# Retention decays moved from q, k and the mask to the values and the result, and the instruction order planned anew

## Chip, cores and metric
One core of a Trainium2 chip. The metric is the device time of one execution in microseconds; the kernel before took 385.36 us (median of 3 runs, 385.14 to 385.75).

## What is computed
Three parts follow each other. Two batches, eight heads of 64, 768 tokens, a model width of 512.

```python
# 1. retention: a state with a decay for each head
gamma = 1.0 - 2.0 ** (-5.0 - np.arange(H))
for t in range(S):
    state = gamma * state + k[:, :, t] (outer) v[:, :, t]
    y[:, :, t] = scale * q[:, :, t] @ state
# 2. spectral mixing
theta = x @ w_theta
zr, zi = x * cos(theta), x * sin(theta)
u = x + w_tok_r @ zr + w_tok_i @ zi            # over the tokens
x2 = u + relu(u @ w_ch)
# 3. gated MLP with a product over the tokens
h = gelu(x2 @ w_in); a, v = halves of h
v_n = (v - mean) / sqrt(var + 1e-6) * g_ln
out = x2 + (a * (w_sg @ v_n + b_sg)) @ w_out
```

## The kernel before
**Tiling.** The 768 tokens of a batch are six chunks of 128; chunk `i` runs from 0 to 11 over both batches, `c` from 0 to 5 in one batch. All large products (angles, mixing, channels, MLP) are done in three terms: each operand is split into an upper part (ScalarE, `split_hi`, L302) and a remainder (VectorE, `split_lo`, L308), and `terms3` multiplies upper by upper, remainder by upper and upper by remainder.

**Retention of one chunk** (`retention`, L426). `load_qk` and `load_kv` bring 512 KB each. `scores` makes k times q for eight heads in two PSUM banks. VectorE multiplies them with a mask that holds scale, decay and causality (L456), scales k by its decay (`fade_k`, L468) and q by its decay, which comes as a block `dqs` of 256 KB for each chunk after the first (L477, L484). `outer` makes k times v, `grow` adds it to the state. `attend` sums the state's part, from the scaled q, and the chunk's part, from the masked scores and v. ScalarE copies the result from PSUM into `xa` or `xb` (L555), and it is split.

**Angles** (`theta`, L576). Twelve products over the four quarters of the model width give the angles of a chunk; the first two quarters use the packed weight `W_THETA`, the last two the weight behind it. ScalarE and VectorE make cosine and sine, PE turns the chunk (`turn`, L650), VectorE multiplies (L658), and the product `z` is split for the token mixing (`mix_main`, `mix_rest`).

**Weights** (`weight`, L343). Each packed weight of 1 MB is loaded into one of two raw buffers, unpacked by ScalarE (L361) and VectorE (L370, L381) and split.

**Order.** Nothing runs in the order of the text. Each step is entered in a `Plan` with an engine, an assumed duration, the buffers it reads and writes and a due time (`prio`). `schedule` (L92) goes through assumed time and gives each engine the ready step with the smallest due time within a short look; the instructions are then issued in that order on each engine, and transfers all from SyncE. The due times come from the constants `C` (L203): chunk `i` is due at `8 + DEL + 13 i`, retention up to `LEAD` earlier, angles `LT` later, mixing `LM` later. `PA` and `AHEAD` bound how far a step may go ahead of its due time. Up to 90 products of `ident` with itself (`keep_warm`, L1109) fill PE in assumed time until 34 us where nothing else is ready.

Of the kernel before, what the change touches and what calls it, by code (L numbers as in the profile page):

```python
# [10 lines left out]
F32 = mybir.dt.float32  # L11
# [21 lines left out]
W_THETA, W_MAIN, W_REST, W_CH, W_INV, W_INU, W_OUT = 0, 2, 8, 11, 13, 15, 17  # L33
N_WP = 19

RAWS, PAIRS, ONES = 2, 35, 7


class Buf:
# [21 lines left out]
class Plan:  # L61
# [5 lines left out]
    def __init__(self, room):  # L67
        self.ops, self.res, self.room = [], {}, room

    def op(self, eng, dur, fn, r=(), w=(), prio=0.0, port=False, after=(), until=None):  # L70
        deps, bufs = set(after), []
        for x in r:
            deps.update(self.res.setdefault(x, ([], []))[0])
        for x in w:
            ws, rs = self.res.setdefault(x, ([], []))
            deps.update(ws)
            deps.update(rs)
        for x in (*r, *w):
            b = x.whole if isinstance(x, Half) else x[0] if isinstance(x, tuple) else x
            if isinstance(b, Buf) and b not in bufs:  # L80
                bufs.append(b)
        o = Op(eng, dur, fn, deps, bufs, prio, port, until)
        for x in r:
            self.res[x][1].append(o)
        for x in w:
            self.res[x] = ([o], [])
        for b in bufs:
            b.users.append(o)
        self.ops.append(o)
        return o  # L90

    def schedule(self, look):  # L92
# [5 lines left out]
        rank, level = {}, {}  # L98
        for k, o in enumerate(self.ops):
            o.missing, o.out = len(o.deps), []  # L100
            level[o] = max([o.prio, *(level[d] for d in o.deps)])
            rank[o] = k
            for d in o.deps:
                d.out.append(o)
# [95 lines left out]
        return sorted(order, key=lambda o: (o.start, rank[o]))  # L200


C = dict(TC=13, LATE=60, AHEAD=20, LM=17, LT=2, LR=16, LW=12, LRW=0, PEL=0.1, DVEL=0.05, ACTL=0.4, CHP=0, SGP=25, RW2=1, PA=30, DEL=6, RS=3.8, LEAD=30, TH=-8, WARM=34.0, NWARM=90, GP=12, LEAD1=15)  # L203


@with_exitstack
def retention_spectral_gmlp(
# [2 lines left out]
    qkv: bass.AP,  # L210
    wts: bass.AP,
    wsg: bass.AP,
    dmask: bass.AP,
    dqs: bass.AP,
    decays: bass.AP,
    gvec: bass.AP,
# [39 lines left out]
    mv = const.tile([P, 3, 4, 2], F32, name="mv")  # L256
    rstd = const.tile([P, 3, 3, 4], F32, name="rstd")
    stats = const.tile([P, 2, 6], F32, name="stats")
    masks = const.tile([P, 2, 512], F32, name="masks")
    dk = const.tile([P, NCH, H], F32, name="dk")  # L260
    states = [const.tile([P, NP * D], F32, name=f"state{n}") for n in range(2)]
    V.memset(states[0], 0.0)
# [23 lines left out]
        return plan.op("PE", dur, fn, **k)  # L286

    def act(words, fn, ps=False, **k):
        return plan.op("ACT", (0.16 if ps else 0.21) + words * 0.83e-3, fn, **k)

    def dve(words, fn, ps=False, fast=False, **k):
        dur = 0.15 + words * (0.52e-3 if fast else 1.042e-3)
# [5 lines left out]
    def dma(kb, fn, **k):  # L298
        return plan.op("SP", kb / 410.0, fn, **k)
# [126 lines left out]
    def retention(i):  # L426
        b, c = divmod(i, NCH)
        t = early(i)
        E, eng = (V, dve) if i < C["GP"] else (G, pool)
        load_qk(i)  # L430
        load_kv(i)
        qk, kv = load[i, 0], load[i, 1]
        if i == 0:
            dma(
                512,
                lambda: nc.sync.dma_start(out=masks, in_=dmask),  # L436
                w=["masks"],
                prio=t - 11.5,
            )
            dma(6, lambda: nc.sync.dma_start(out=dk, in_=decays), w=["dk"], prio=t - 11.2)  # L440
        sc = [bank(), bank()]

        def scores():
# [4 lines left out]
                    cols = slice(p * P, (p + 1) * P)  # L448
                    mm(ap(sc[h])[:, cols], k[rows, cols], q[rows, cols], True, True)

        pe(0.93, scores, r=[qk], w=sc, prio=t)
        at[i] = Buf("pair")
        for h in range(2):

            def mask(h=h):
                V.tensor_tensor(  # L456
                    out=ap(at[i])[:, h * 512 : (h + 1) * 512],
                    in0=ap(sc[h]),
                    in1=masks[:, h],
                    op=ALU.mult,  # L460
                )

            dve(512, mask, ps=True, r=[sc[h], "masks"], w=[(at[i], h)], prio=t + 1)
        if c < NCH - 1:

            def fade_k(G=E):
                k3 = ap(kv)[:, 0:512].rearrange("p (h d) -> p h d", h=H)
                G.tensor_tensor(  # L468
                    out=k3, in0=k3, in1=dk[:, c, :, None].to_broadcast([P, H, D]), op=ALU.mult
                )  # L470

            eng(512, fade_k, r=[kv, "dk"], w=[(kv, 0)], prio=t + 1)
        if c > 0:
            dq, qd = Buf(), Buf()
            dma(
                256,
                lambda: nc.sync.dma_start(out=ap(dq), in_=dqs[c - 1]),  # L477
                w=[dq],
                prio=t - 8,
                after=[gate[i - 2]] if i >= 2 else (),  # L480
            )
            eng(
                512,
                lambda: E.tensor_tensor(  # L484
                    out=ap(qd), in0=ap(qk)[:, 0:512], in1=ap(dq), op=ALU.mult
                ),
                r=[qk, dq],
                w=[qd],
                prio=t + 1.5,
            )  # L490
        state, state_next = states[c % 2], states[(c + 1) % 2]
        if c < NCH - 1:
            kp = bank()

            def outer():
                kk, vv = ap(kv)[:, 0:512], ap(kv)[:, 512:1024]
                for p in range(NP):
                    for h in range(2):
                        rows = slice(h * D, (h + 1) * D)
                        cols = slice(p * P + h * D, p * P + (h + 1) * D)  # L500
                        mm(ap(kp)[rows, p * D : (p + 1) * D], kk[:, cols], vv[:, cols], True, True)

            pe(0.5, outer, r=[(kv, 0), kv], w=[kp], prio=t + 2)

            def grow():
                add = ap(kp)[:, 0 : NP * D]
                if c == 0:
                    V.tensor_copy(out=state_next, in_=add)
                else:
                    V.tensor_tensor(out=state_next, in0=add, in1=state, op=ALU.add)  # L510

            dve(
                256,
                grow,
                ps=True,
                r=[kp] + ([("state", c % 2)] if c else []),
                w=[("state", (c + 1) % 2)],
                prio=t + 2.5,
            )
        xp = bank()  # L520

        def attend():
            vv, a = ap(kv)[:, 512:1024], ap(at[i])
            if c > 0:
                for p in range(NP):
                    cols = slice(p * P, (p + 1) * P)
                    for h in range(2):
                        rows = slice(h * D, (h + 1) * D)
                        mm(
                            ap(xp)[rows, cols],  # L530
                            state[rows, p * D : (p + 1) * D],
                            ap(qd)[rows, cols],
                            p == 0,
                            False,
                        )
# [9 lines left out]
                        c == 0 or p == NP - 1,  # L545
                    )

        r = [kv, (at[i], 0), (at[i], 1)]
        if c > 0:
            r += [qd, ("state", c % 2)]  # L550
        gate[i] = pe(0.93 if c == 0 else 1.85, attend, r=r, w=[xp], prio=t + 3)
        keys = [("x", b, c, d) for d in range(NP)]
        act(
            512,
            lambda: A.activation(  # L555
                out=x_chunk(i),
                in_=ap(xp).rearrange("p (n t) -> p n t", n=NP),
                func=AF.Copy,
            ),
            ps=True,  # L560
            r=[xp],
            w=keys,
            prio=t + 5,
        )
# [11 lines left out]
    def theta(i):  # L576
# [1 line left out]
        t = T(i) + C['LT']  # L578
        th = bank()

        def angle():
            xh, xl = (ap(x, F32R) for x in xhl[i])
            terms3(
                ap(th),
                [
                    (
                        (xh[:, k * P : (k + 1) * P], xl[:, k * P : (k + 1) * P]),
                        w_tile(W_THETA + k // 2, k % 2),
                    )
                    for k in range(NP)  # L590
                ],
            )

        pe(
            2.75,
            angle,
            r=[*xhl[i], *wp[W_THETA], *wp[W_THETA + 1]],
            w=[th],
            prio=t,
        )  # L600
        kk = Buf(dtype=I32)
        z, zh, zl = Buf("pair"), Buf("pair", F32R), Buf("pair", F32R)
        co, r = Half(z, 0), Half(z, 1)
# [47 lines left out]
                    out=ap(tp)[:, p * P : (p + 1) * P], in_=x_chunk(i)[:, p], identity=ident  # L651
                )

        pe(0.5, turn, r=keys, w=[tp], prio=t + 5.3)

        def times():
            z2 = ap(z).rearrange("p (n t) -> p n t", n=2)
# [466 lines left out]
def _decays():  # L1124

    g = 1.0 - 2.0 ** (-5.0 - np.arange(H, dtype=np.float64))
    t = np.arange(P, dtype=np.float64)
    scale = 1.0 / math.sqrt(D)  # L1130
    m = np.zeros((P, 2, 512), np.float64)
    dq = np.zeros((NCH - 1, P, 512), np.float64)
    dk = np.zeros((P, NCH, H), np.float64)
    low = (t[None, :] >= t[:, None]).astype(np.float64)
    dist = np.maximum(t[None, :] - t[:, None], 0.0)
    for p in range(NP):
        cols = slice(p * P, (p + 1) * P)
        for h in range(2):
            gh = g[2 * p + h]
            m[:, h, cols] = scale * low * gh**dist  # L1140
            for c in range(NCH):
                dk[:, c, 2 * p + h] = gh ** (P - 1.0 - t - P * (c + 1.0))
                if c:
                    dq[c - 1, h * D : (h + 1) * D, cols] = scale * gh ** (t + 1.0 + P * c)
    return m.astype(np.float32), dq.astype(np.float32), dk.astype(np.float32)


def _tok_tiles(w):
# [66 lines left out]
```

## Time and profile before
| | |
|---|---|
| median of 3 runs | 385.36 us |
| the profiled execution | 385.82 us |
| its span, first to last instruction | 384.0 us |
| granted clock of TensorE, mean | 0.999 |
| busy: PE, VectorE, ScalarE | 378.7, 276.5, 167.6 us |
| bytes read from memory | 38.43 MB |

PE's busy time counts products that compute nothing (`keep_warm`) too. Start times below are microseconds from the span's start.

### The profile page before, as it was taken

Reading aid. Unit: us, or ns where it says so; the run is one execution under the profiler, and the core shown is the slowest. Engines: PE = TensorE matmul, PEld = TensorE weight load, DVE = VectorE, ACT = ScalarE, POOL = GpSimd, SP = SyncE. Lnnn points to the kernel's source line nnn. Section 1 sums busy time; section 2 is a strip of 40 time slices with the busy share of each in tenths; the row PEclk is TensorE's granted clock in tenths of the full one; section 3 lists DMA queues with packets and bytes.
Section 4 is the critical chain, followed back from the end, with each engine's and each line's share of the span. In section 5 each row is a group of like instructions: output and inputs, shape, how many; then the busy total and the mean of one; then the engine's idle time right before and its main releaser. Section 6 shows DMA issues by size and latency. Waiting matters only on the chain.

```text
span 384.0 us, 5887 instructions
## 1 busy us (share of the span) xinstructions
PE 378.7 (99%) x2456; PEld 322.8 (84%) x2456; DVE 276.5 (72%) x412; ACT 167.6 (44%) x240; POOL 3.0 (1%) x8
## 2 busy tenths in 40 slices
PE   8899999999999999999999999999999999999996
PEld 8887888887988988788898888888888888998885
DVE  2888998988988836698835555989799996554222
ACT  1437566655624444567123213777685812111000
POOL 0000000000000000000000000020000000000000
PEclk9999999999999999999999999999999999999999
DMA  7995545634267530008000000540000000000223
GB/s 293 408 366 224 219 153 203 249 157 145 111 218 247 191 111 3 2 12 342 4 0 2 0 0 16 172 184 2 0 0 2 0 1 2 0 2 29 109 86 106
DMA packets 11786, 41.95 MB, mean 109 GB/s; under 512 B 1520, under 2 KB 2544, under 8 KB 9328
## 3 DMA queue, kind: packets, MB, share of 16 engines
q1 hardware_dynamic: 11760, 41.58, 28.9%
q8 instruction: 19, 0.31, 0.3%
q14 instruction: 7, 0.06, 0.0%
HBM read 38.43 MB, written 3.15 MB: 108 GB/s over the span
## 4 chain that ended last, share of the span: by engine, by line
PE 94%; DMA 3%; SPq 1%; issue 0%; DVE 0%
PE b L283 93%; DMA b<-qkv 3%; PE b L650 1%; SPq L348 0%; SPq L416 0%; SPq L405 0%; DVE b L1029 0%; SPq L440 0%; SPq L436 0%
## 5 line engine op out<-in xcount | busy, mean ns | idle before, releaser
L283 PE MATMUL b<-b,b 128*128 128x512 f32 (+2 forms) x1788 | 332.5, 352 | 0.0
L283 PEld LDWEIGHTS b<-b,b 128*128 128x128 f32 (+1 forms) x1788 | 278.0, 183 | 47.8 <-issue 2.6
L302 ACT ACTIVATE b<-b 128x1024 fp32r<-128x1024 f32 (+1 forms) x64 | 54.1, 863 | 57.2 <-DVE b L977 35.5
L308 DVE TENSOR_TENSOR b<-b,b 128x512 fp32r<-128x512 f32 (+1 forms) x64 | 59.0, 945 | 12.4 <-ACT b L302 11.2
L381 DVE SCALAR_TENSOR_TENSOR b<-b 128x1024 int32<-128x1024 int32 x38 | 46.5, 1223 | 0.8
L361 ACT ACTIVATE b<-b 128x1024 f32<-128x1024 f32 x19 | 22.2, 1166 | 11.8 <-DMA b<-wts 11.8
L302 ACT ACTIVATE b<-xa 128x512 fp32r<-128x512 f32 x24 | 14.9, 629 | 22.3 <-DVE xa L779 12.0
L308 DVE TENSOR_TENSOR b<-xa,b 128x512 fp32r<-128x512 f32 x24 | 16.3, 689 | 11.2 <-ACT b L302 11.1
L283 PE MATMUL b<-b 64*128 64x128 f32 (+1 forms) x352 | 20.4, 258 | 1.1 <-DMA b<-qkv 1.1
L283 PEld LDWEIGHTS b<-b 64*128 64x128 f32 (+1 forms) x352 | 17.3, 164 | 4.8 <-issue 3.1
L456 DVE TENSOR_TENSOR b<-b,masks 128x512 f32<-128x512 f32 x24 | 15.6, 684 | 6.6 <-PE b L283 6.6
L791 ACT ACTIVATE b<-b 128x512 f32<-128x512 f32 x24 | 13.8, 591 | 13.1 <-PE b L283 12.2
L658 DVE TENSOR_TENSOR b<-b,b 128x1024 f32<-128x1024 f32 x12 | 14.6, 1221 | 6.3 <-PE b L650 6.3
L815 DVE SCALAR_TENSOR_TENSOR b<-b,b 128x512 f32<-128x512 f32 x24 | 15.9, 678 | 2.1 <-ACT b L809 2.0
L809 ACT ACTIVATE b<-b 128x512 f32<-128x512 f32 x24 | 14.6, 627 | 4.4 <-DVE b L799 4.4
L799 DVE SCALAR_TENSOR_TENSOR b<-b,b 128x512 f32<-128x512 f32 x24 | 15.5, 675 | 1.3 <-ACT b L791 1.3
L970 DVE SCALAR_TENSOR_TENSOR b<-b,gcol,brow 128x512 f32<-128x512 f32 x12 | 9.0, 749 | 10.1 <-PE b L283 9.9
L992 DVE TENSOR_TENSOR b<-b,xa 128x512 f32<-128x512 f32 x8 | 5.5, 691 | 14.2 <-PE b L283 14.2
L302 ACT ACTIVATE b<-xb 128x512 fp32r<-128x512 f32 x12 | 7.4, 631 | 18.0 <-DVE xb L737 9.5
L370 DVE TENSOR_SCALAR b<-b 128x1024 int32<-128x1024 int32 x19 | 13.1, 688 | 2.3 <-DMA b<-wts 2.3
L606 ACT ACTIVATE b<-b 128x512 int32<-128x512 f32 x12 | 7.2, 597 | 16.3 <-PE b L283 16.3
L626 ACT ACTIVATE b<-b 128x512 f32<-128x512 f32 x12 | 7.5, 628 | 13.3 <-DVE b L615 13.3
(49 smaller groups left out, 178.2 us busy)
## 6 DMA issues: line engine op xcount, KB each, us to landing
b<-wts SPq DMA_DIRECT2D x19, 1024.0 KB, 5.2
b<-qkv SPq DMA_DIRECT2D x24, 512.0 KB, 6.5
out<-b SPq DMA_DIRECT2D x11, 256.0 KB, 2.0
b<-dqs SPq DMA_DIRECT2D x10, 256.0 KB, 6.7
b<-wsg SPq DMA_DIRECT2D x9, 256.0 KB, 7.7
masks<-dmask SPq DMA_DIRECT2D x1, 512.0 KB, 4.1
brow<-bvec SPq DMA_DIRECT2D x1, 384.0 KB, 4.9
out<-b SPq DMA_DIRECT2D x2, 128.0 KB, 1.7
```

Source lines behind the costliest of these rows:

```text
L283: nc.tensor.matmul(out=o, lhsT=l, rhs=r, start=start, stop=stop)
L302: act(words, lambda: A.activation(out=hi(), in_=src(), func=AF.Copy), prio=prio, r=r, **k)
L308: lambda: E.tensor_tensor(out=lo(), in0=src(), in1=hi().bitcast(F32), op=ALU.subtract),
L361: lambda: A.activation(out=words(1).bitcast(F32), in_=words(1).bitcast(F32), func=AF.Copy, scale=REBIAS),
L370: lambda: V.tensor_scalar(out=words(0), in0=words(0), scalar1=29, scalar2=None, op0=ALU.logical_shift_right),
L381: lambda scalar=scalar, op=op: V.scalar_tensor_tensor(out=words(0), in0=words(1), scalar=scalar, in1=words(0), op0=op, op1=ALU.bitwise_or,),
L456: V.tensor_tensor(out=ap(at[i])[:, h * 512 : (h + 1) * 512], in0=ap(sc[h]), in1=masks[:, h], op=ALU.mult,)
L658: V.tensor_tensor(out=z2, in0=ap(tp)[:, None, :].to_broadcast([P, 2, 512]), in1=z2, op=ALU.mult)
L791: lambda: A.activation(out=ap(s), in_=ap(t), func=AF.Square),
L799: lambda: V.scalar_tensor_tensor(out=ap(s), in0=ap(s), scalar=1.0 / GA, in1=ap(t), op0=ALU.add, op1=ALU.mult),
L809: lambda: A.activation(out=ap(s), in_=ap(s), func=AF.Tanh, scale=GA * GC),
L815: lambda: V.scalar_tensor_tensor(out=ap(o), in0=ap(s), scalar=1.0, in1=ap(t), op0=ALU.add, op1=ALU.mult),
```

## The change
The decays leave q, k and the mask. The values of a chunk are scaled by `g ** -t`, with `t` counted from the start of the batch, before both `outer` and `attend`; the result is multiplied by `scale * g ** t`, a block `dqs` of 256 KB that is now loaded for all six chunks, the first included. The mask is one causal block of 128x128, made on the chip (two GpSimd instructions) and repeated over the heads by its access pattern; the load of 512 KB goes. For chunks 0 to 7 (`FA=8`) ScalarE scales the values, in eight instructions, one for each head; for 8 to 11 VectorE does it in one. VectorE makes the result from PSUM where ScalarE copied it. The angle products stand as two steps, each of which waits for its own weight alone. There is one more pair buffer (36). Assumed durations, `C` and the meaning of a step's level (`lev`) are new, so the order is.

```diff
-C = dict(TC=13, LATE=60, AHEAD=20, LM=17, LT=2, LR=16, LW=12, LRW=0, PEL=0.1, DVEL=0.05, ACTL=0.4, CHP=0, SGP=25, RW2=1, PA=30, DEL=6, RS=3.8, LEAD=30, TH=-8, WARM=34.0, NWARM=90, GP=12, LEAD1=15)
+C = dict(TC=13, LATE=90, AHEAD=60, LM=28, LT=9, LR=16, LW=15, LRW=15, PEL=0.1, DVEL=0.1, ACTL=0.7, CHP=5, SGP=10, RW2=0, PA=25, DEL=6, RS=3.8, LEAD=40, TH=-8, WARM=34.0, NWARM=90, FA=8, LEAD1=5)
...
-    masks = const.tile([P, 2, 512], F32, name="masks")
+    causal = const.tile([P, P], F32, name="causal")
+    G.memset(causal, 1.0)
+    G.affine_select(
+        out=causal, in_=causal, pattern=[[1, P]], compare_op=ALU.is_ge, fill=0.0, base=0,
+        channel_multiplier=-1,
+    )
...
-        pe(0.93, scores, r=[qk], w=sc, prio=t)
+        pe(1.06, scores, r=[qk], w=sc, prio=t)
...
-                    in1=masks[:, h],
+                    in1=causal[:, None, :].to_broadcast([P, NP, P]),
...
-            eng(512, fade_k, r=[kv, "dk"], w=[(kv, 0)], prio=t + 1)
...
+        def fade_v():
+            v3 = ap(kv)[:, 512:1024].rearrange("p (h d) -> p h d", h=H)
+            V.tensor_tensor(
+                out=v3, in0=v3, in1=dk[:, c, :, None].to_broadcast([P, H, D]), op=ALU.mult
+            )
+        def fade_v_heads():
+            for h in range(H):
+                v = ap(kv)[:, 512 + h * D : 512 + (h + 1) * D]
+                A.activation(out=v, in_=v, func=AF.Copy, scale=dk[:, c, h : h + 1])
+        k = dict(r=[kv, "dk"], w=[(kv, 1)], prio=t + 1)
+        if i < C["FA"]:
+            plan.op("ACT", 1.95, fade_v_heads, **k)
+        else:
+            dve(512, fade_v, **k)
...
-        act(
-            512,
-            lambda: A.activation(
+        dve(
+            512,
+            lambda: V.tensor_tensor(
                 out=x_chunk(i),
-                in_=ap(xp).rearrange("p (n t) -> p n t", n=NP),
-                func=AF.Copy,
+                in0=ap(xp).rearrange("p (n t) -> p n t", n=NP),
+                in1=ap(dq).rearrange("p (n t) -> p n t", n=NP),
+                op=ALU.mult,
             ),
...
+        for half in range(2):
+            def angle(half=half):
...
+            pe(1.37, angle, r=[*xhl[i], *wp[W_THETA + half]], w=[th], prio=t + 0.01 * half, lev=t)
```

## Rows read from the trace of the kernel before

**Rows 1.** The page, busy time of each engine.
```profile
PE 378.7 (99%) x2456; PEld 322.8 (84%) x2456; DVE 276.5 (72%) x412; ACT 167.6 (44%) x240; POOL 3.0 (1%) x8
```
**Rows 2.** Chain of waits in order of time: start, duration, what.
```profile
4.54 13.44 DMA b<-qkv
...
172.08 208.89 PE b L283 x1068
```
**Rows 3.** Waits of PE's weight loads, 24 to 381 us: total, times, longest.
```profile
PEld b L283 <- issue: 5.9, 27, 0.4
```
**Rows 4.** PE's timeline, 0 to 50 us: start, duration, line, operands, count.
```profile
4.92 1.16 PE L283 MATMUL b<-b 64*128 64x128 f32 x16
6.01 2.05 PE L283 MATMUL b<-ident 128*128 128x128 f32 x16
...
11.07 5.97 PE L283 MATMUL b<-ident 128*128 128x128 f32 x52
18.11 1.78 PE L283 MATMUL b<-b 64*128 64x128 f32 x32 [1.07 <-DMA b<-qkv]
19.82 2.50 PE L283 MATMUL b<-ident 128*128 128x128 f32 x20
...
23.34 0.49 PE L283 MATMUL b<-ident 128*128 128x128 f32 x2
23.76 1.09 PE L283 MATMUL b<-b,state 64*64 64x128 f32 x16
...
26.27 3.02 PE L283 MATMUL b<-b,b 128*128 128x512 f32 x12
...
38.40 8.46 PE L283 MATMUL b<-b,b 128*128 128x512 f32 x36
```
**Rows 5.** Windows of the head: busy of each engine, clock, DMA share, GB/s.
```profile
10.00:20.00 10.00, 8.93 (x101) 8.46 (x99) 8.16 (x11) 3.84 (x4) 0.00 (x0) 1.00 1.02 409
```
**Rows 6.** VectorE's timeline, 0 to 48 us.
```profile
7.73 0.69 DVE L468 TENSOR_TENSOR b<-b,dk 128x512 f32<-128x512 f32 x1 [0.33 <-DMA b<-qkv]
...
19.07 1.22 DVE L308 TENSOR_TENSOR b<-b,b 128x1024 fp32r<-128x1024 f32 x1
...
22.88 1.22 DVE L308 TENSOR_TENSOR b<-b,b 128x1024 fp32r<-128x1024 f32 x1
...
39.62 1.23 DVE L308 TENSOR_TENSOR b<-b,b 128x1024 fp32r<-128x1024 f32 x1 [0.34 <-ACT b L302]
```
**Rows 7.** ScalarE's timeline, 0 to 48 us.
```profile
11.44 1.22 ACT L361 ACTIVATE b<-b 128x1024 f32<-128x1024 f32 x1 [1.05 <-DMA b<-wts]
16.72 1.18 ACT L361 ACTIVATE b<-b 128x1024 f32<-128x1024 f32 x1 [4.06 <-DMA b<-wts]
...
31.38 0.60 ACT L555 ACTIVATE xa<-b 128x512 f32<-128x512 f32 x1
31.87 0.72 ACT L633 ACTIVATE b<-b,halfpi 128x512 f32<-128x512 f32 x1
```
**Rows 8.** Windows: busy PE, PEld, DVE, ACT, POOL, clock, DMA share, GB/s.
```profile
30.00:60.00 30.00, 30.00 (x250) 24.08 (x248) 28.98 (x36) 19.23 (x27) 0.00 (x0) 1.00 0.51 195
```
**Rows 9.** Instructions by line and shape: count, busy us, mean ns, idle before.
```profile
L302 ACT ACTIVATE b<-b 128x1024 fp32r<-128x1024 f32 x31 | 34.5, 1119 | 21.7 <-DVE b L381 9.0 <-DVE b L658 7.4 <-PE b L283 3.1
L302 ACT ACTIVATE b<-b 128x512 fp32r<-128x512 f32 x33 | 19.5, 624 | 35.5 <-DVE b L977 35.5
L456 DVE TENSOR_TENSOR b<-b,masks 128x512 f32<-128x512 f32 x24 | 15.6, 684 | 6.6 <-PE b L283 6.6
...
L900 ACT ACTIVATE b<-b,rstd 128x512 f32<-128x512 f32 x12 | 8.8, 805 | 3.8 <-DVE rstd L889 3.8
L633 ACT ACTIVATE b<-b,halfpi 128x512 f32<-128x512 f32 x12 | 8.7, 725 | 0.4
...
L468 DVE TENSOR_TENSOR b<-b,dk 128x512 f32<-128x512 f32 x10 | 6.8, 684 | 0.3 <-DMA b<-qkv 0.3
...
L555 ACT ACTIVATE xa<-b 128x512 f32<-128x512 f32 x8 | 4.8, 600 | 16.3 <-PE b L283 16.2
```

More of the change, by code (lines that the diff above doesn't have):

```diff
@@ L34 @@
 N_WP = 19
-RAWS, PAIRS, ONES = 2, 35, 7
+RAWS, PAIRS, ONES = 2, 36, 7
 class Buf:
@@ L68, in __init__, with op @@
         self.ops, self.res, self.room = [], {}, room
-    def op(self, eng, dur, fn, r=(), w=(), prio=0.0, port=False, after=(), until=None):
+    def op(self, eng, dur, fn, r=(), w=(), prio=0.0, port=False, after=(), until=None, lev=None):
         deps, bufs = set(after), []
@@ L82, in op @@
         o = Op(eng, dur, fn, deps, bufs, prio, port, until)
+        o.lev = prio if lev is None else lev
         for x in r:
@@ L100, in schedule @@
             o.missing, o.out = len(o.deps), []
-            level[o] = max([o.prio, *(level[d] for d in o.deps)])
+            level[o] = max([o.lev, *(level[d] for d in o.deps)])
             rank[o] = k
@@ L212, in retention_spectral_gmlp @@
     wsg: bass.AP,
-    dmask: bass.AP,
     dqs: bass.AP,
@@ L288, in act @@
     def act(words, fn, ps=False, **k):
-        return plan.op("ACT", (0.16 if ps else 0.21) + words * 0.83e-3, fn, **k)
+        dur = 0.21 + words * 0.83e-3 if words < 1024 else 0.085 + words * 1.06e-3
+        return plan.op("ACT", dur - (0.04 if ps else 0.0), fn, **k)
     def dve(words, fn, ps=False, fast=False, **k):
@@ L428, in retention @@
         t = early(i)
-        E, eng = (V, dve) if i < C["GP"] else (G, pool)
         load_qk(i)
@@ L433, in retention @@
         if i == 0:
-            dma(
-                512,
[L436 to L440, printed above, removed]
+            dma(6, lambda: nc.sync.dma_start(out=dk, in_=decays), w=["dk"], prio=t - 11.5)
         sc = [bank(), bank()]
@@ L456, in mask @@
                 V.tensor_tensor(
-                    out=ap(at[i])[:, h * 512 : (h + 1) * 512],
-                    in0=ap(sc[h]),
-                    in1=masks[:, h],
+                    out=ap(at[i])[:, h * 512 : (h + 1) * 512].rearrange("p (n t) -> p n t", n=NP),
+                    in0=ap(sc[h]).rearrange("p (n t) -> p n t", n=NP),
+                    in1=causal[:, None, :].to_broadcast([P, NP, P]),
                     op=ALU.mult,
                 )
-            dve(512, mask, ps=True, r=[sc[h], "masks"], w=[(at[i], h)], prio=t + 1)
@@ L464, in retention @@
[L464 to L470, printed above, removed]
-            eng(512, fade_k, r=[kv, "dk"], w=[(kv, 0)], prio=t + 1)
[L473 to L480, printed above, removed]
-            )
[L482 to L490, printed above, removed]
+            dve(512, mask, ps=True, r=[sc[h]], w=[(at[i], h)], prio=t + 1)
@@ L491, in retention @@
+        if i < C["FA"]:
+            plan.op("ACT", 1.95, fade_v_heads, **k)
+        else:
+            dve(512, fade_v, **k)
+        dq = Buf()
+        dma(
+            256,
+            lambda: nc.sync.dma_start(out=ap(dq), in_=dqs[c]),
+            w=[dq],
+            prio=t - 8,
+            after=[gate[i - 2]] if i >= 2 else (),
+        )
         state, state_next = states[c % 2], states[(c + 1) % 2]
@@ L501, in outer @@
                         mm(ap(kp)[rows, p * D : (p + 1) * D], kk[:, cols], vv[:, cols], True, True)
-            pe(0.5, outer, r=[(kv, 0), kv], w=[kp], prio=t + 2)
+            pe(0.58, outer, r=[(kv, 1), kv], w=[kp], prio=t + 2)
             def grow():
@@ L531, in attend @@
                             state[rows, p * D : (p + 1) * D],
-                            ap(qd)[rows, cols],
+                            ap(qk)[rows, cols],
                             p == 0,
@@ L546, in attend @@
                     )
-        r = [kv, (at[i], 0), (at[i], 1)]
+        r = [kv, (kv, 1), (at[i], 0), (at[i], 1)]
         if c > 0:
-            r += [qd, ("state", c % 2)]
-        gate[i] = pe(0.93 if c == 0 else 1.85, attend, r=r, w=[xp], prio=t + 3)
+            r += [qk, ("state", c % 2)]
+        gate[i] = pe(0.95 if c == 0 else 1.9, attend, r=r, w=[xp], prio=t + 3)
         keys = [("x", b, c, d) for d in range(NP)]
-        act(
+        dve(
             512,
-            lambda: A.activation(
+            lambda: V.tensor_tensor(
                 out=x_chunk(i),
-                in_=ap(xp).rearrange("p (n t) -> p n t", n=NP),
-                func=AF.Copy,
+                in0=ap(xp).rearrange("p (n t) -> p n t", n=NP),
+                in1=ap(dq).rearrange("p (n t) -> p n t", n=NP),
+                op=ALU.mult,
             ),
             ps=True,
-            r=[xp],
+            r=[xp, dq],
             w=keys,
@@ L579, in theta @@
         th = bank()
[L581 to L600, printed above, removed]
+        for half in range(2):
+            def angle(half=half):
+                xh, xl = (ap(x, F32R) for x in xhl[i])
+                terms3(
+                    ap(th),
+                    [
+                        (
+                            (xh[:, k * P : (k + 1) * P], xl[:, k * P : (k + 1) * P]),
+                            w_tile(W_THETA + half, k % 2),
+                        )
+                        for k in (2 * half, 2 * half + 1)
+                    ],
+                    half == 0,
+                    half == 1,
+                )
+            pe(1.37, angle, r=[*xhl[i], *wp[W_THETA + half]], w=[th], prio=t + 0.01 * half, lev=t)
         kk = Buf(dtype=I32)
@@ L652, in turn @@
                 )
-        pe(0.5, turn, r=keys, w=[tp], prio=t + 5.3)
+        pe(0.46, turn, r=keys, w=[tp], prio=t + 5.3)
         def times():
@@ L1128, in _decays @@
     g = 1.0 - 2.0 ** (-5.0 - np.arange(H, dtype=np.float64))
[L1129 to L1145, printed above, removed]
+    t = np.arange(S, dtype=np.float64).reshape(NCH, 1, P) + 1.0
+    dq = np.zeros((NCH, 2, D, NP, P), np.float64)
+    dq += g.reshape(NP, 2).T[None, :, None, :, None] ** t[:, :, None, None, :] / math.sqrt(D)
+    dk = g ** -t.transpose(2, 0, 1)
+    return dq.reshape(NCH, P, 512).astype(np.float32), dk.astype(np.float32)
 def _tok_tiles(w):
@@ L1193 @@
     )
-    masks, dqs, dk = _decays()
+    dqs, dk = _decays()
     arrays = {
@@ L1198 @@
         "wsg": np.ascontiguousarray(np.concatenate(_tok_tiles(x["moe2_w_sg"]), axis=0)),
-        "dmask": masks,
         "dqs": dqs,
```

## The prediction
> **What bounds the kernel now.** I read the page first: PE is busy for 99% of the span and every other engine much less [rows 1]. The chain of waits in order of time says the same more sharply: one transfer of q and k that lands at 17.98 us, then PE work to 380.97, then an addition of 0.42 us and a store [rows 2]. PE's waits from 24 to 381 us are an empty list (its weight loads pause 27 times for 5.9 us [rows 3], which is what changing between the small and the large products costs), so behind 24 us no faster engine can shorten anything; only products taken away, or PE started earlier, can.
>
> So the third view is PE's timeline of the head [rows 4]. There "busy" misleads: the products named `b<-ident` are the filler of `keep_warm`, which computes nothing. They take 2.05 us from 6.01, the stretch 11.07 to 18.11 (with 1.07 us of plain waiting at its end), 2.50 us from 19.82 and 23.34 to 23.76: 2.05 + 7.04 + 2.50 + 0.42 = 12.0 us. With the 4.92 us before the first scores, PE has lost 16.9 us by 23.76 and nothing after it. The change adds and removes no matmul (scores, outer, attend, 12 products for each angle and the turns keep their number), so its time is: what it does to the 12.0 us, plus any stall that it makes behind 24 us.
>
> **Loads.** SP issues them in order, and in the head they run near 400 GB/s [rows 5]. `dmask` (512 KB) goes, a `dqs` block of chunk 0 (256 KB) comes in front of the first large weight or just behind it. At the 409 GB/s of 10 to 20 us 512 KB take 1.28 us and 256 KB 0.64. So k, v of chunk 0, for which DVE waited until 7.73 [rows 6], land some 1.2 us earlier, and all behind `dqs` about 0.6 earlier: k, v of chunk 1, the second angle weight (before at 16.72 [rows 7]) and q, k of chunk 2 (17.98 to 17.3). SP gains two issues and loses one, while its queue is ahead of the transfers: nothing. Later the second batch's extra block (256 KB) meets DMA engines that are half idle (share 0.51 in [rows 8]): nothing.
>
> **VectorE.** It loses 10 scalings of k and 10 of q, of one size (0.684 us [rows 9]) and gains 12 products of result and decay (PSUM and a tile, as L456: 0.684) and 4 scalings of v (0.684, as L468, also with a broadcast operand): 20 x 0.684 - 16 x 0.684 = 2.7 us less, 13 x 0.684 - 8 x 0.684 = 3.4 us less in the eight first chunks. The mask product stays; its mask is now one block repeated over four, and L468 repeats an operand at the same 0.68 us, so 0 (bounds 0 and 0). In 30 to 60 us DVE is busy 29.0 of 30 [rows 8], so this is welcome there but hidden under PE.
>
> **ScalarE.** It loses 12 copies of the result (0.60 us) and gains 64 scalings of 128x64 with a scale read from a tile. No such row exists. From 512 and 1024 columns (0.624 and 1.119 us [rows 9]) the slope is 0.97 ns a column and the fixed part 0.13, so 64 columns cost 0.19; an operand read from a tile adds 0.10 (L633, 0.725, against L302, 0.624) and two of them 0.18 (L900, 0.805). A following instruction starts some 0.1 us before the end of the one before it (31.38 + 0.60 against 31.87 [rows 7]). Eight of them so take between 8 x 0.19 = 1.5 (no operand cost, no overlap) and 8 x 0.37 = 3.0 us; the middle figures give 8 x (0.29 - 0.1) + 0.1 = 1.6, and I take 2.0, towards the middle of the bounds. Per chunk that is 2.0 - 0.6 = 1.4 us more, 11 us over eight chunks, where ScalarE is busy 19.2 of 30 us [rows 8]: hidden.
> The Trainium skill (ScalarE: Activation LUTs, What ACT_TABLE_LOAD costs) gives 186 ns plus 0.833 ns a column, 93 for a pointer operand and 93 of overlap; by it eight cost an estimated 2.0 us, and the sum would not move. Its section Rules for kernel authors says to put multiplications on VectorE, not ScalarE, which speaks against this part; its price is in the third rival.
>
> **The head, step by step** (one DVE or ACT instruction of 512 columns 0.6 to 0.7).
> 1. Scores 0 end at 6.01 as before. k, v of chunk 0 land at 6.5, the eight scalings end at 8.5; attend 0 now waits for them too (before it began at 7.99). Scores 1 can go first. Result 0 waits for `dqs` and goes through DVE, so turn 0 (0.5 us) falls behind 11.07. Lost until 11.07: 2.05 + 0.5 = 2.5 us.
> 2. k, v of chunk 1 lie between the weights that land at 11.44 and 16.72 [rows 7] and are a third of the bytes: 13.2, less 0.6, is 12.6. ScalarE waits 4.06 us up to 16.72, from 12.66 [rows 7], so values 1 are ready at 14.6. Outer and attend, together 2.5 us (23.76 to 26.27 [rows 4], no longer waiting for a scaled q), run 14.7 to 17.3. From 11.07 to 17.3 that leaves 6.2 - 2.5 - 0.5 (turn 0) = 3.2 us lost.
> 3. Scores 2 run 17.3 to 18.4. The first angle half needs only the first weight, ready at 20.3 before (L308 at 19.07 [rows 6]); it gains 0.6 from the loads, and up to 3 if its upper part no longer stands behind the second weight's first instruction on ScalarE (16.72 [rows 7]). I take 18.6. Angle 0's first half (1.4 us) fills part of 18.4 to 21.5: 1.7 us lost.
> 4. From 21.5 there are the first half of angle 1, scores 3, outer 2, attend 2, both second halves (second weight before at 24.1 [rows 6]): 8 us of work, by when chunk 2's angle follows.
> Lost: 2.5 + 3.2 + 1.7 = 7.4 instead of 12.0, a gain of 4.6. But the queues are in order: a late landing holds everything behind it (before, 1.07 us at 18.11 and 4.06 on ScalarE). New waits of this kind: result on DVE for `dqs` and attend, with weight and mask work behind it; values on ScalarE for k, v, with the weights' upper parts behind them. One such slip, about that 1.07 us, I take off: 3.5 us. Bounds: 0 (each second of slip eats its second) and 7 (only the 4 to 5 us until k, v of chunk 1 stay lost).
> **Halves.** Twelve more places where small products may cut in, at 5.9 / 27 = 0.22 us a pause [rows 3]: from 0 to 2.6 us. Halves mostly follow each other once both weights are there: 0.3.
> **Sum.** The profiled execution took 385.82 us (span 384.0 and 1.8 around it); 385.82 - 3.5 + 0.3 = 382.6. It stood 0.46 above the median of the runs, so 382.2 for the median.
>
> **Rivals.**
> *The gain is given back.* PE, 3.5 us ahead, needs real work at 35 to 45 us. In the 36 products from 38.40 [rows 4] the last 24 are the main mix of chunk 0; they begin at about 41.2, and its operand was ready at 40.84 (39.62 + 1.23 [rows 6]): just in time. If that is not earlier, PE waits there what it won: 385. Against it: the second half of angle 0 comes earlier, and LEAD = 40 brings chunks 4 and 5 forward as other work.
> *DVE becomes the bound, slower.* Result chunks now stand in DVE's queue at 29.0 of 30 us busy [rows 8], behind weights, where a ScalarE with room made them. If eight chunks each make PE wait 1 us the time is 382.2 + 8 = 390; it decides from 3.2 / 8 = 0.4 us a chunk. Against it: 3.4 us less DVE work in those chunks, and PE's empty list of waits with more.
> *ScalarE holds the values, slower.* With 3.0 us a chunk instead of 2.0 outer and attend of chunks 0 to 2 slip by 1 us each and the weights' upper parts with them: 3.5 - 3 leaves 0.5, 385; with 4 us it is 388. The skill's rule named above is this rival; ScalarE idle for 4 us at the place [rows 7] speaks against it.
> *More is won.* No slip, first weight at 17: 7 us, 378.4.
>
> **How the numbers follow.** This measurement tells 0.2% (0.8 us) from no change. Forecast, 1 to 6 us faster: 0.62; more won: 0.07; given back: 0.12; DVE slower: 0.12; ScalarE: 0.07, most of it slower. Faster 0.70, same 0.12, slower 0.18. The likeliest one's own range is 379.5 to 384.4; with part of the rivals on both sides 378.5 to 387.0.
>
> **What would show it.** PE's timeline: attend 1 by about 17 us instead of 23.76, a first angle product before 20 instead of 26.27, filler stretches of about 7 us in sum, and from 22 us no wait of PE. The eight scalings near 2.0 us a chunk, k, v of chunk 0 waited for until 6.5. The prediction is wrong if PE's list of waits has entries behind 24 us (DVE L308 or the result product as releaser), if the filler still sums to 11 us, or if the tail behind PE's last product grows beyond its 3 us.

## The result, and the profile after

The changed kernel takes 381.68 us (median of 4 runs, 381.43 to 382.85), the kernel before, measured beside it, 385.56 us: a ratio of 0.9901, 95% interval 0.9888 to 0.9914, 3.9 us faster. The forecast was 382.2 us in 378.5 to 387.0. The profiled execution is the slowest of the four (382.85 us, span 381.1; the others have spans of 379.7 to 380.0), so the trace below shows 2.9 us of the 3.9. In the comparisons of the experiments a difference between two ratios is turned into time with 385.6 us.

The page's busy times, to be set against [rows 1]: VectorE has 2.5 us less, ScalarE 7.4 us more, and PE 4.0 us less although no product was taken out. What PE lost is filler.

```profile
PE 374.7 (98%) x2422; PEld 318.4 (84%) x2422; DVE 274.0 (72%) x408; ACT 175.0 (46%) x292; POOL 4.3 (1%) x10
```

The chain of waits in order of time (start, duration, what), against [rows 2]: it now goes through two loads of q and k, hangs on a load until 21.88 us, and then is PE to 378.13.

```profile
2.15 6.71 DMA b<-qkv
...
8.87 13.01 DMA b<-qkv
...
22.01 17.31 PE b L290 x216
...
169.25 208.88 PE b L290 x1068
```

A chain that begins its PE part later (22.01 instead of 18.11) and yet ends earlier is the point of this case: what counts is how much real work is done by then. PE's timeline of the head, against [rows 4]:

```profile
5.02 1.16 PE L290 MATMUL b<-b 64*128 64x128 f32 x16
6.11 1.83 PE L290 MATMUL b<-ident 128*128 128x128 f32 x14
8.99 1.78 PE L290 MATMUL b<-b 64*128 64x128 f32 x32 [1.04 <-DMA b<-qkv]
10.59 1.04 PE L290 MATMUL b<-b,b 128*64 128x128 f32 x16
11.57 4.06 PE L290 MATMUL b<-ident 128*128 128x128 f32 x34
15.56 0.69 PE L290 MATMUL b<-b 128*64 128x64 f32 x16
16.18 1.09 PE L290 MATMUL b<-b,state 64*64 64x128 f32 x16
17.20 1.09 PE L290 MATMUL b<-b,b 128*64 128x128 f32 x16
18.78 1.16 PE L290 MATMUL b<-b 64*128 64x128 f32 x16 [0.49 <-DMA b<-qkv]
19.88 0.66 PE L648 MATMUL b<-ident,xa 128*128 128x128 f32 x4
20.37 1.06 PE L290 MATMUL b<-ident 128*128 128x128 f32 x8
22.01 1.78 PE L290 MATMUL b<-b 64*128 64x128 f32 x32 [0.59 <-DMA b<-qkv]
23.72 1.67 PE L290 MATMUL b<-b,b 128*128 128x512 f32 x6
```

Filler (`b<-ident`) and waits take 6.11 to 8.99, 11.57 to 15.56, 0.49 us before 18.78 and 20.37 to 22.01: 2.88 + 3.99 + 0.49 + 1.64 = 9.0 us, where it was 12.0. With the first scores 0.1 us later that is 2.9 us, the whole difference of the two spans. Attend of chunk 1 (`b<-b,state`) stands at 16.18 instead of 23.76. From 24 to 378 us PE's list of waits is empty, as before, and the 3.0 us behind its last product are the same.

### The profile page after: what moved, and what is told of

It is laid out like the page before. It is cut to its first block, busy times and chain, and to the rows that moved or that the text cites. A ratio compares the mean times of both kernels' runs of the same rounds, so it can differ in the third digit from the quotient of the medians.

```text
span 381.1 us, 5873 instructions
## 1 busy us (share of the span) xinstructions
PE 374.7 (98%) x2422; PEld 318.4 (84%) x2422; DVE 274.0 (72%) x408; ACT 175.0 (46%) x292; POOL 4.3 (1%) x10
## 4 chain that ended last, share of the span: by engine, by line
PE 93%; DMA 5%; SPq 0%; DVE 0%; issue 0%
PE b L290 92%; DMA b<-qkv 5%; PE b L648 1%; DVE b L1027 0%; SPq L424 0%; SPq L441 0%; SPq L413 0%
## 5 line engine op out<-in xcount | busy, mean ns | idle before, releaser
L310 ACT ACTIVATE b<-b 128x1024 fp32r<-128x1024 f32 (+1 forms) x64 | 53.2, 859 | 66.7 <-DVE b L975 38.2
L316 DVE TENSOR_TENSOR b<-b,b 128x1024 fp32r<-128x1024 f32 (+1 forms) x64 | 59.3, 955 | 9.7 <-ACT b L310 9.5
L290 PEld LDWEIGHTS b<-b 64*128 64x128 f32 (+1 forms) x352 | 17.3, 164 | 7.0 <-issue 2.8
L457 DVE TENSOR_TENSOR b<-b,causal 128x512 f32<-128x512 f32 x24 | 15.7, 684 | 8.2 <-PE b L290 8.2
L789 ACT ACTIVATE b<-b 128x512 f32<-128x512 f32 x24 | 13.8, 590 | 14.7 <-PE b L290 14.7
L475 ACT ACTIVATE b<-b,dk 128x64 f32<-128x64 f32 x64 | 16.1, 336 | 8.7 <-DMA b<-qkv 8.7
L807 ACT ACTIVATE b<-b 128x512 f32<-128x512 f32 x24 | 14.7, 629 | 6.2 <-DVE b L797 6.1
## 6 DMA issues: line engine op xcount, KB each, us to landing
brow<-bvec SPq DMA_DIRECT2D x1, 384.0 KB, 7.7
```

The source lines that it names most:

```text
L290: nc.tensor.matmul(out=o, lhsT=l, rhs=r, start=start, stop=stop)
L310: act(words, lambda: A.activation(out=hi(), in_=src(), func=AF.Copy), prio=prio, r=r, **k)
L316: lambda: E.tensor_tensor(out=lo(), in0=src(), in1=hi().bitcast(F32), op=ALU.subtract),
L457: V.tensor_tensor(out=ap(at[i])[:, h * 512 : (h + 1) * 512].rearrange("p (n t) -> p n t", n=NP), in0=ap(sc[h]).rearrange("p (n t) -> p n t ...
L475: A.activation(out=v, in_=v, func=AF.Copy, scale=dk[:, c, h : h + 1])
L789: lambda: A.activation(out=ap(s), in_=ap(t), func=AF.Square),
```

## Experiments

Each ratio is to the kernel before, measured beside the run. The changed kernel's own ratio is 0.9901 (0.9888 to 0.9914).

**The old constants.** `C` as it was, with `FA=8`.

```diff
-C = dict(TC=13, LATE=90, AHEAD=60, LM=28, LT=9, ..., LEAD=40, ..., FA=8, LEAD1=5)
+C = dict(TC=13, LATE=60, AHEAD=20, LM=17, LT=2, ..., LEAD=30, ..., FA=8, LEAD1=15)
```

> The changed kernel with the constants of the order as they were before (FA stays 8). Theory (the moved decays shorten the head): 34 filler products are issued instead of 29, 5 x 0.22 = 1.1 us more lost in the head, no wait of TensorE behind 24 us: about 382.8 us. Rival (the new order brings the gain): about 385 us.

385.06 us, ratio 0.9986 (0.9978 to 0.9995): nearly all of the gain is gone, and my theory of a head that the moved decays shorten by themselves falls as far as the time goes. PE's timeline shows where:

```profile
15.56 1.09 PE L290 MATMUL b<-b,state 64*64 64x128 f32 x16
...
18.70 1.66 PE L290 MATMUL b<-b,b 128*128 128x512 f32 x6
...
34.30 2.25 PE L290 MATMUL b<-ident 128*128 128x128 f32 x16
...
37.99 5.51 PE L290 MATMUL b<-b,b 128*128 128x512 f32 x23 [0.39 <-DVE b L316]
```

The head did become shorter: attend 1 at 15.56, the first angle half at 18.70. But at 34.30 the plan has nothing real for PE, 2.2 us of filler follow, and then a wait for a remainder that VectorE splits. That is the prediction's first rival, the gain given back at 35 to 45 us, near its place. These 2.6 us aren't all: up to 24 us this head loses some 4.7 us less than the kernel before, and the span is only 0.9 us shorter (383.1 against 384.0), so about 1.2 us more is given back at places that I didn't find.

**The new order alone.** The kernel before, with the new `C` and the new assumed durations.

```diff
-C = dict(TC=13, LATE=60, AHEAD=20, LM=17, LT=2, ..., LEAD=30, ..., GP=12, LEAD1=15)
+C = dict(TC=13, LATE=90, AHEAD=60, LM=28, LT=9, ..., LEAD=40, ..., GP=12, LEAD1=5)
-        pe(0.93, scores, r=[qk], w=sc, prio=t)
+        pe(1.06, scores, r=[qk], w=sc, prio=t)
...
```

> The kernel before with the new constants and the new assumed durations, decays where they were. Theory: 45 filler products instead of 46, attend of chunk 1 still waits for the scaled q, so 385 us, within 0.7 of before. Rival (the new order brings the gain): 382 us.

390.68 us, ratio 1.0121 (1.0102 to 1.0140): slower than before by 1.2%, outside what either theory gave. The head is as before (attend 1 at 23.97 us). The loss is a new one, in PE's timeline near 175 us (3.1 of the 3.7 us by which this run's span, 387.7 us, is longer than before):

```profile
172.68 6.08 PE L283 MATMUL b<-b,b 128*128 128x512 f32 x24 [0.64 <-DVE b L309]
181.19 1.20 PE L283 MATMUL b<-b,b 128*128 128x512 f32 x4 [2.43 <-DVE b L309]
```

What VectorE does just ahead of the longer wait is to unpack a weight (its remainder follows at 179.93):

```profile
177.03 2.98 DVE L382 SCALAR_TENSOR_TENSOR b<-b 128x1024 int32<-128x1024 int32 x2
```

Neither half of the change brings the gain alone: the moved decays win it in the head, the order keeps it behind the head, and without the moved decays that order makes PE wait for VectorE. That the scalings of q and k cause this wait isn't shown: from 160 to 182 us VectorE's timeline has none of them. It is busier around it than in the changed kernel (34.95 of the 40 us from 140 to 180 against 33.04, and 28.78 before), but this run also lacks the changed kernel's 36th pair buffer, its halves of the angles and its new levels.

**Whole angles.** The twelve products of a chunk as one step.

```diff
-        for half in range(2):
-            def angle(half=half):
...
+        pe(2.74, angle, r=[*xhl[i], *wp[W_THETA], *wp[W_THETA + 1]], w=[th], prio=t)
```

> The changed kernel with each angle as one step again. Theory: 33 filler products instead of 29, the first angle starts some 2 us later, 0.5 to 1 us slower than the changed kernel: about 382.5 us. Rival (the halves are worth nothing, since other work is ready by then): 381.7 us.

383.02 us, ratio 0.9933 (0.9921 to 0.9946): the halves are worth 0.0032, 1.2 us. A stretch of filler stands where the first half of angle 0 stood:

```profile
22.64 1.26 PE L290 MATMUL b<-ident 128*128 128x128 f32 x8
```

**Padded decays.** The rows of the decay table from 192 to 512 bytes.

```diff
-    dk = const.tile([P, NCH, H], F32, name="dk")
+    dk = const.tile([P, 16, H], F32, name="dk")
...
+    dk = np.concatenate([dk, np.zeros((P, 16 - NCH, H))], axis=1)
```

> The changed kernel with the rows of the decay table padded from 192 to 512 bytes; its place in the queue stays. Theory (the 192-byte packets slow the loads beside them between 3 and 5.5 us): k, v of chunk 0 land near 6.7 us instead of 7.66, all behind by 0.5 to 1 us earlier, 381 us. Rival (the dip has another cause): 7.7 us again and 381.7 us.

381.91 us, ratio 0.9911 (0.9897 to 0.9925), k, v of chunk 0 are waited for until 7.96 us, and between 3 and 6 us the loads move 283, 209 and 201 GB/s in the three one-us windows: the small packets are not the cause of the low rate. The theory falls.

**The old constants with LEAD = 40.**

> The changed kernel with the constants of before, but LEAD = 40 as in the change. Theory (with the old LEAD of 30 chunk 4 comes too late to fill TensorE at 34 to 38 us, which gave the gain back): 27 filler products instead of 34, no filler stretch and no wait of TensorE between 34 and 38 us, 383 us. Rival (the loss there comes from VectorE's order, whatever the chunk): filler or a wait stays there and the time is 385 us.

```diff
-C = dict(..., LEAD=30, ...)
+C = dict(..., LEAD=40, ...)
```

384.58 us, ratio 0.9979 (0.9965 to 0.9992): little better than with 30. Four filler records still stand at 36.26, and behind them products wait for VectorE (0.63 us at 39.03). The rival is right: it isn't the due time of chunk 4 alone. The trace is of the slowest of the seven executions (386.22 us), and in it TensorE's granted clock fell at these pauses: its mean was 0.80 from 38 to 40 us and 0.50, the lower level, from 40 to 42 us (the number ahead of the DMA share), where an attend's sixteen products with the state took 1.90 us instead of 1.09:

```profile
40.92 1.90 PE L290 MATMUL b<-b,state 64*64 64x128 f32 x16
40.00:42.00 2.00, 2.00 (x13) 1.35 (x13) 1.90 (x3) 1.42 (x3) 0.00 (x0) 0.50 0.75 274
```

**The new order with LEAD = 30.**

```diff
-C = dict(..., LEAD=40, ...)
+C = dict(..., LEAD=30, ...)
```

> The changed kernel with LEAD = 30 alone. Theory: 31 filler products instead of 29 and chunks 4 and 5 later, 0.4 us or more lost: 382.2 to 383 us. Rival (LEAD does nothing by itself): 381.7 us.

384.92 us, ratio 0.9981 (0.9971 to 0.9991): this one constant takes back 0.0080, 3.1 us, much more than I expected. The list of PE's waits behind 24 us (total, times, longest), empty in the changed kernel, has an entry, one part of it at 38.86 us:

```profile
PE b L290 <- DVE b L316: 1.2, 2, 0.6
```

These waits are 1.2 of the 3.1 us; the rest isn't broken down. So LEAD = 40 is needed in the new order, and in the old one it isn't enough.

**All values on VectorE.**

```diff
-C = dict(..., FA=8, LEAD1=5)
+C = dict(..., FA=0, LEAD1=5)
```

> The changed kernel with FA = 0: VectorE scales the values of all chunks, in one instruction of 0.68 us instead of eight on ScalarE of 2.0 us. Theory (VectorE is the busier one in 20 to 60 us): 33 filler products instead of 29, 1 to 2 us slower, 383 us. Rival (ScalarE's eight instructions hold up outer and attend, as in the prediction's third rival): 1 us faster, 380.7 us.

383.55 us, ratio 0.9946 (0.9934 to 0.9958): 0.0045, 1.7 us slower than with ScalarE. The longer filler stretch in front of outer 1, and one that the changed kernel doesn't have:

```profile
11.84 4.73 PE L290 MATMUL b<-ident 128*128 128x128 f32 x40
...
24.25 1.47 PE L290 MATMUL b<-ident 128*128 128x128 f32 x6
```

Eight instructions on the engine that has room beat one of a third of their time on the busier one.

**Weights later.** `TH` moves the load and unpacking of the two angle weights behind those of chunk 2.

```diff
-C = dict(..., TH=-8, ...)
+C = dict(..., TH=-3, ...)
```

> The changed kernel with TH = -3: the two angle weights (1 MB each) are loaded and unpacked after q, k, v of chunk 2 instead of around those of chunk 1. Theory (the head waits for transfers, and 1.25 MB of a chunk bring 3.5 us of products at once while 2 MB of weights bring none until they are unpacked): 25 filler products instead of 29, 0.9 us faster, 380.8 us. Rival (angles then come late and their chain to the mixing starves TensorE at 35 to 50 us): 382 us or more, with waits of TensorE there.

382.41 us, ratio 0.9923 (0.9910 to 0.9937): no faster than the changed kernel, and 0.0022 (0.8 us) slower with intervals that overlap. Attend 1 comes at 14.06, but PE then waits for the weights:

```profile
22.15 2.50 PE L290 MATMUL b<-ident 128*128 128x128 f32 x20
```

The rival is right in kind: the first angle half comes at 24.40 instead of 23.72, and one wait of 0.6 us for VectorE appears behind the head (it ends at 157.8 us).

**Weights around chunk 2's values.** The same with `TH=-4`.

> The changed kernel with TH = -4: the first angle weight is loaded just ahead of k, v of chunk 2, the second behind them. Theory (the 2 MB of weights between the chunks are what the head waits for): 22 filler products instead of 29, 1 us faster, 380.7 us. Rival (as with TH = -3 the first angles come later by what attend gained, and the order behind them meets new stalls): 381.7 to 382.5 us.

```diff
-C = dict(..., TH=-8, ...)
+C = dict(..., TH=-4, ...)
```

382.15 us, ratio 0.9910 (0.9897 to 0.9923): not told apart from the changed kernel, with the same wait of 0.6 us. Its trace has 46 filler records instead of 58, six products fewer, and they brought nothing that can be measured.

**The mask's load put back.** 512 KB that nobody reads, in the old place of the mask.

```diff
+            dma(
+                512,
+                lambda: nc.sync.dma_start(
+                    out=xb[:, 0:2].rearrange("p n b t -> p (n b t)"), in_=qkv[0, 1, 0]
+                ),
+                prio=t - 11.6,
+            )
```

> The changed kernel with a load of 512 KB put back where the mask's load was (q and k of another chunk, into space that is written later; nobody reads it). Theory (each 512 KB ahead in the queue delays all that follows by 1.28 us): k, v of chunk 0 land at 8.9 us instead of 7.66, 34 filler products instead of 29, 1.0 to 1.3 us slower, 382.9 us. Rival (the low rate between 3 and 6 us, not the bytes, sets the landings, as k, v of chunk 0 landed no earlier without the mask): same landings, 381.7 us.

383.60 us, ratio 0.9956 (0.9944 to 0.9967), 0.0055 or 2.1 us slower; but the landings didn't move as the theory said. ScalarE's first scaling, which waits for k, v of chunk 0, begins at 7.45 us, against 7.66 without the load:

```profile
7.45 2.02 ACT L482 ACTIVATE b<-b,dk 128x64 f32<-128x64 f32 x8 [5.38 <-DMA b<-qkv]
```

One-us windows of this run (the last number is GB/s) show how: the load passes at 414 and 362 in a time in which the changed kernel moves far less (shown below).

```profile
3.00:4.00 1.00, 1.00 (x7) 1.00 (x7) 0.00 (x0) 0.00 (x0) 0.00 (x0) 1.00 1.02 414
4.00:5.00 1.00, 1.00 (x9) 0.88 (x10) 0.00 (x0) 0.00 (x0) 0.00 (x0) 1.00 1.13 362
```

So the loss isn't in this landing. Part of it is in the order: the plan counts the load's time, and the order that comes out has a wait of 0.7 us for VectorE near 158 us that the changed kernel hasn't. Behind its first angle half (23.29 us) this run takes 358.5 us, the changed kernel 357.4 (381.1 - 23.72). In the head the plan sets 34 filler products instead of 29, but the last of them end at 20.8 us, and PE then still waits for a load of q and k:

```profile
21.58 1.78 PE L290 MATMUL b<-b 64*128 64x128 f32 x32 [0.76 <-DMA b<-qkv]
...
158.85 1.43 PE L290 MATMUL b<-b,b 128*128 128x512 f32 x5 [0.65 <-DVE b L316]
```

That the five more products cost their 5 x 0.22 = 1.1 us isn't shown.

**Decays first.** The decay table as the very first transfer.

```diff
-w=["dk"], prio=t - 11.5
+w=["dk"], prio=t - 12.5
```

> The changed kernel with the decay table loaded as the very first transfer, ahead of q, k of chunk 0. Theory (the low rate between 3 and 6 us comes with the decay table): the low rate comes at 2 to 4 us, q, k of chunk 0 land up to 1 us later than 5.0 us and k, v of chunk 0 at 7.5 us or before. Rival (the low rate stands at its time or with k, v whatever goes ahead): q, k at 5.1 us, the low rate again at 3 to 6 us, 381.7 us.

381.54 us, ratio 0.9893 (0.9879 to 0.9908), not told apart from the changed kernel. k, v of chunk 0 come at 6.65 us, one earlier, and scores 0 start at 5.40; of the low rate, 197 GB/s at 5 to 6 us stays. Half of each theory, and the cause stays open. In the runs that begin with the same four loads as the changed kernel, k, v of chunk 0 are waited for until 7.04 (the old constants) to 8.31 us (the new order with LEAD = 30): 6.65 lies outside this scatter, the 7.45 with the load put back inside it and far from the 8.9 that the bytes would give.

**No filler.**

```diff
-C = dict(..., NWARM=90, ...)
+C = dict(..., NWARM=0, ...)
```

> The changed kernel with no filler products (NWARM = 0). Theory (filler costs nothing, its stretches are waits for data): the same start of each real product within 0.3 us, 381.5 us if the granted clock stays at 1.0. Rival (without work in the head the granted clock falls there and products take up to twice their time until it is back): clock under 1.0 in some window of the first 30 us and 383 us or more.

384.09 us (383.46 to 388.34), ratio 0.9978 (0.9956 to 1.0001): slower by 0.0077, 3.0 us, and far less even. One line of PE and two windows of the head (the number ahead of the DMA share is the granted clock):

```profile
9.07 3.13 PE L290 MATMUL b<-b 64*128 64x128 f32 x32 [3.25 <-DMA b<-qkv]
8.00:9.00 1.00, 0.00 (x0) 0.00 (x0) 0.00 (x0) 1.00 (x5) 0.00 (x0) 0.50 1.06 446
10.00:20.00 10.00, 8.29 (x112) 6.92 (x109) 8.00 (x11) 6.09 (x14) 0.00 (x0) 0.78 1.02 409
```

Within PE's wait of 3.25 us the clock fell to 0.50, the lower level, between 8 and 9 us, and scores 1 with what follows took 3.13 us instead of 1.78. So the filler isn't free to leave out. How much of the 3.0 us is the clock's isn't shown: without the filler the plan also makes another order (turn 0 stands ahead of outer 1), the first angle half begins at 23.65 us, as early as in the changed kernel's trace, and near 170 us PE waits 0.8 us for VectorE and 0.7 for ScalarE. In the changed kernel, with waits of 1.04, 0.49 and 0.59 us between filler, the clock stays at 1.00 in every window of the head.

## Why the prediction was right, step by step

**The bound.** Right. PE has no wait behind 24 us in either kernel, and the spans differ by what the heads differ. Of the signs that the prediction named, attend 1 (16.18 us), the filler stretches (1.83 + 4.06 + 1.06 = 6.95 us) and the scalings (2.02 us) came as it said; the first angle product (23.72 us, not before 20) and the landing of k, v of chunk 0 (7.66 us, not 6.5) didn't.

**Step 1, chunk 0.** The time that it gives (2.5 us lost) is near the 2.9 measured, but by luck, since its reason failed: k, v of chunk 0 don't land at 6.5 us. ScalarE's timeline of the changed kernel has them at 7.66, as good as before [rows 6]:

```profile
7.66 2.02 ACT L475 ACTIVATE b<-b,dk 128x64 f32<-128x64 f32 x8 [5.60 <-DMA b<-qkv]
11.40 1.20 ACT L369 ACTIVATE b<-b 128x1024 f32<-128x1024 f32 x1 [1.72 <-DMA b<-wts]
13.33 2.02 ACT L475 ACTIVATE b<-b,dk 128x64 f32<-128x64 f32 x8 [0.74 <-DMA b<-qkv]
15.26 1.13 ACT L310 ACTIVATE b<-b 128x1024 fp32r<-128x1024 f32 x1
```

I had priced the mask's bytes at the 409 GB/s of [rows 5]. In one-us windows the changed kernel moves much less than that just there:

```profile
3.00:4.00 1.00, 1.00 (x7) 1.00 (x7) 0.00 (x0) 0.00 (x0) 0.00 (x0) 1.00 0.87 220
4.00:5.00 1.00, 1.00 (x7) 0.90 (x6) 0.00 (x0) 0.00 (x0) 0.00 (x0) 1.00 0.88 169
5.00:6.00 1.00, 1.00 (x17) 0.97 (x16) 0.00 (x0) 0.00 (x0) 0.00 (x0) 1.00 0.89 287
```

In the kernel before, the mask passed at the full rate first, and the low rate came later and was shorter:

```profile
3.00:4.00 1.00, 1.00 (x7) 1.00 (x6) 0.00 (x0) 0.00 (x0) 0.00 (x0) 1.00 1.02 414
4.00:5.00 1.00, 1.00 (x9) 0.88 (x8) 0.00 (x0) 0.00 (x0) 0.00 (x0) 1.00 0.98 283
5.00:6.00 1.00, 1.00 (x16) 0.89 (x16) 0.00 (x0) 0.00 (x0) 0.00 (x0) 1.00 0.68 192
```

The run with the load put back shows the same from the other side: the bytes cost this landing nothing. What that load costs lies elsewhere, half of it in the order behind the head.

**Step 2, chunk 1.** Right in mechanism. Values 1 take 2.02 us from 13.33; I had 2.0 from 12.6. Outer and attend of chunk 1 run 15.56 to 18.3 instead of 14.7 to 17.3, and 4.0 us are lost before them instead of 3.2. By the same view ScalarE did have the room: it waited for loads before both scalings, and the first weight's upper part (15.26) stands ahead of the second weight, which step 3 had hoped for.

**Step 3, the first angle half.** Mis-placed. VectorE's timeline:

```profile
18.32 1.22 DVE L316 TENSOR_TENSOR b<-b,b 128x1024 fp32r<-128x1024 f32 x1
19.46 2.48 DVE L389 SCALAR_TENSOR_TENSOR b<-b 128x1024 int32<-128x1024 int32 x2
21.86 0.68 DVE L316 TENSOR_TENSOR b<-xa,b 128x512 fp32r<-128x512 f32 x1
```

The weight was ready at 19.54, 0.9 us after my 18.6, but the remainder of result 0 stood behind the second weight's unpacking and came at 22.54; the half ran at 23.72, not at 18.6. The stretch it should have filled lost 1.64 us; that I had 1.7 was luck, since I had it for another reason. The halves still brought 1.2 us, at 22 to 24.

**The sum of the head.** Lost: 9.0 us against 7.4 plus a slip of 1.1, 8.5. Halves: 26 pauses of 6.1 us in the weight loads instead of 27 of 5.9 [rows 3], so 0.2 for the 0.3.

```profile
PEld b L290 <- issue: 6.1, 26, 0.4
```

The trace is of the slowest execution, and two other runs show where its last microsecond lies. The padded decays and the decays first have the same order of products on PE, and spans of 380.2 and 379.9 us, close to those of the other executions of the changed kernel (379.7 to 380.0). Their first angle halves:

```profile
22.80 1.65 PE L290 MATMUL b<-b,b 128*128 128x512 f32 x6
22.47 1.66 PE L290 MATMUL b<-b,b 128*128 128x512 f32 x6
```

From there to the end all three take the same 357.4 us (380.2 - 22.80, 379.9 - 22.47, 381.1 - 23.72). So the difference is in the head: there PE's list of waits for q and k is 2.1 us in the changed kernel's trace, nothing in the first of these runs and 0.4 in the second. The one slip of 1.07 us that I took off was a guess at something that changes from execution to execution, and its size came near by luck.

**The prices of the engines.** By line and shape (count, busy, mean ns, idle before):

```profile
L475 ACT ACTIVATE b<-b,dk 128x64 f32<-128x64 f32 x64 | 16.1, 336 | 8.7 <-DMA b<-qkv 8.7
L457 DVE TENSOR_TENSOR b<-b,causal 128x512 f32<-128x512 f32 x24 | 15.7, 684 | 8.2 <-PE b L290 8.2
...
L554 DVE TENSOR_TENSOR xa<-b,b 128x512 f32<-128x512 f32 x8 | 5.5, 686 | 1.9 <-PE b L290 1.9
```

The repeated mask costs nothing (684 ns, as in [rows 9]) and the result product 686. One scaling takes 336 ns where my rows gave 290; eight in a row take 2.02 us. The Trainium skill's figures (ScalarE: Activation LUTs, What ACT_TABLE_LOAD costs) give an estimated 186 + 53 + 93 = 332 ns; this trace, with 336, agrees.

**The rivals.** *Given back* didn't happen in the changed kernel, but it is what happens with the old constants, at 34 us; my reason against it (LEAD) was half right, since LEAD = 30 alone costs 3.1 us and LEAD = 40 alone saves almost nothing in the old order. *VectorE becomes the bound* didn't happen, since PE has no wait; how near it is, the new order alone shows, with 3.1 us of waits for VectorE, and four variants of the changed kernel with 0.6 to 1.2 us (LEAD = 30, the two with later weights, the load put back). *ScalarE holds the values* is refuted by the run with all values on VectorE, 1.7 us slower. The rule of the Trainium skill to keep multiplications off ScalarE (ScalarE: Activation LUTs, Rules for kernel authors) gives the speed per element as its reason; in this kernel it doesn't hold, since what counts here is which engine has room.

**What stays open.** Which of the constants beside LEAD keep the gain; why the new order makes PE wait for VectorE when the decays aren't moved; and what lowers the rate of the first loads, since neither the packet size nor the table's place settles it.

## What to carry to other kernels

On a kernel whose busiest engine shows 99%, first take the filler out of that number: the loss was 12 us in the first 24, and the gain could only come from there. A gain at the head lasts only if the order behind it has other real work at the point where PE arrives early, so an algebraic change and a re-plan have to be measured together, and apart: here they gave -0.1% and +1.2% alone and -1.0% together. And where a plan sets the order, a load has two prices, its bytes and what the plan makes of it: the load put back left k, v of chunk 0 where they were and still cost 2.1 us, about half of it in what follows the head.

## What was not expected of the hardware

The loads of the first microseconds don't all run at the rate of the later ones: in the changed kernel 169 to 287 GB/s between 3 and 6 us against 409 at 10 to 20, in the kernel before 414 at 3 to 4 us and 192 to 283 at 4 to 6. 512 KB put in front of k, v of chunk 0 left its landing at 7.45 us instead of 7.66.

TensorE's granted clock fell to 0.50, the lower of its levels, within a wait of 3.25 us in the run without filler, and waits of up to 1.04 us between filler left it at 1.00 in the changed kernel. But it also fell to 0.50 in one execution with the old constants and LEAD = 40, where the longest wait ahead of it was 0.63 us, next to a few shorter pauses. So these runs give no length of a wait that is safe.
